# Attention and multiplicative FFN in one kernel: the fifth group turned by DMA, and every engine's order written as a list

## The chip, the cores and the metric

The kernel runs on one core of one Trainium2 chip. The metric is the time of one execution in device microseconds; a lower number is better. TensorE is called PE in the views, VectorE DVE, ScalarE ACT, GpSimd POOL and SyncE SP.

## The reference, cut to what matters

```python
q, k: 8 batches x 12 heads x 448 tokens x 64, float32; v the same
q_n = q / sqrt(mean(q*q) + 1e-6) * g_q          # k_n likewise with g_k
attn = softmax((q_n @ k_n.T) / 8)               # per head, 448 x 448
x = (attn @ v) as 3584 tokens x 768
h = ((x @ w1) * (x @ w2)) @ w3                  # 1024 wide
out = h @ w_out                                 # 3584 x 768, float32
```

## The kernel before, in words

The 96 heads go in 24 groups of four heads; three groups make a batch. A group's queries and keys are loaded (`load_qk`, L384), squared on ACT (L487), summed on DVE (L492), turned into a factor by a logarithm and an exponential on ACT (L501, L504) and scaled to bf16 on DVE (L526, two halves for queries and two for keys). They must then be turned so that the head dimension lies on partitions. That is done in one of two ways. For the first `N_PE_T = 5` groups it is done by PE: `do_turn` issues seven 128x128 transposes for the queries and seven for the keys (L1163) into a PSUM bank, and ACT or DVE copies the bank to `qkT` (L369, L373, L375), multiplying the queries by the weights `g_col` on the way. For the other 19 groups it is done by DMA: `send` (L600) issues one transposing DMA for queries and one for keys on SP's queue, and `by_g` (L534) multiplies the queries by `g_col` on DVE.

The scores of a group are seven passes (`do_score`, L716) of two PSUM banks each; ACT takes the exponential of each (L738). A pass is four concurrent matmuls over quarters of the array. When all seven are there, the value products follow, for one group or for two at once (`start_pv`, L782 and L803); ACT makes the reciprocal of the sums (L825, L826) and DVE multiplies (L845). The FFN works in pairs of PSUM banks (`Pair`, `do_pass`, L908): w pairs (w3 and w_out multiplied once into `w34s`), f pairs (x by w1, copied by ACT or DVE; x by w2, multiplied with that copy by DVE at L989 into `abT`) and o pairs (`abT` by `w34s`, copied and stored). In each pair the two row halves of the array swap banks once or more: `hand_over` (L892) puts an empty instruction on SP or POOL that waits for the last pass of the first half, and the first pass of the second half waits for it.

w3 also has to be turned by PE (`do_w3_turn`, L1185, eight transposes per block). Before there is real work PE is kept busy with warm matmuls on zeros: 512 columns (`warm`, L1360) and then 256 columns (`do_warm`, L1233).

A planner in Python runs through the whole kernel with assumed durations while the program is built and so fixes the order of instructions on every engine. On PE the rules in `pe_try` choose the next step; on ACT, DVE, SP and POOL the planner takes the job that could start first, ties by a key. The built program has no choice left: each engine executes its instructions in the written order, and semaphores hold it where data are not there.

Of the kernel before, what the change touches and what calls it, by code (L numbers as in the profile page):

```python
# [21 lines left out]
TO_ENGINE = 0.23  # L22
TO_ENGINE_WIDE = 0.45
DRAIN = 0.11
LAG = {"ACT": 0.11, "DVE": 0.09, "SP": 0.0, "POOL": 0.0}
# [3 lines left out]
BUSY = 75.0  # L29


class Job:
# [4 lines left out]
    def __init__(self, engine, took, key, emit, needs=(), done=None, moves=None):  # L37
        self.took = took if isinstance(took, dict) else {engine: took}
        self.key, self.emit, self.needs, self.done = key, emit, needs, done
        self.moves, self.any = moves, isinstance(took, dict)  # L40
# [5 lines left out]
class Planner:  # L46
# [3 lines left out]
    def __init__(self):  # L50
        self.free = {e: 0.0 for e in ("ACT", "DVE", "SP", "POOL", "PE")}
        self.jobs = []
# [5 lines left out]
    def add(self, *args, **kw):  # L58
        self.jobs.append(Job(*args, **kw))
# [37 lines left out]
    def commit(self, job, start, engine):  # L97
# [3 lines left out]
        self.jobs.remove(job)  # L101
# [28 lines left out]
    def run(self, pe_step, finished):  # L130

        stuck = 0
        while not finished() or self.jobs:
            best = None
            behind = {
                e: sum(
                    job.took[e]
                    for job in self.jobs
                    if e in job.took
                    and not job.any  # L140
                    and job.ready() <= max(self.free[e], self.now) + 0.3
                )
                for e in ("ACT", "DVE")
            }
            for e in ("ACT", "DVE", "SP", "POOL"):
                mine = []
                for job in self.jobs:
                    if e not in job.took:
                        continue
                    ready = job.ready()  # L150
                    if job.moves is not None:
                        ready = max(ready, self.lane_free(e))
                    if ready < INF:
                        at = max(ready, self.free[e], self.now)
                        if job.any and any(
                            max(ready, self.free[x], self.now) + job.took[x] + behind[x]
                            < at + job.took[e] + behind[e]
                            for x in job.took
                        ):
                            continue  # L160
                        mine.append((at, job.key, job))
                if not mine:
                    continue
                first = min(m[0] for m in mine)
                start, _, job = min(
                    (m for m in mine if m[0] <= first + 1e-9), key=lambda m: m[1]
                )
                if best is None or start < best[0]:
                    best = (start, job, e)
# [26 lines left out]
def kernel(  # L196
# [42 lines left out]
    N_PE_T = 5  # L239
# [4 lines left out]
    PAIRS = (2, 3)  # L244
    MARGINS = (0.267, 0.281)
    LOWS = (0, 2)
    VALUE_BANKS = (6, 6)
    HOLD = 0
    SOONS = (2, 4)
    STARVES = (6, 5)  # L250
    HUNGERS = (0.632, 0.85)
    ONES = (0, 0)
    FULL = (0.765, 0.208)
    PARTS = ((2, 4, 6, 8), (2, 4, 6, 8), (4, 8))
    EARLY_PAIRS = 3
    AHEAD_W3 = 3
    EARLY = 4
    STOCKS = (17, 14)
    PACES = (1.289, 1.754)
# [4 lines left out]
    SCALE_ON_ACT = ()  # L264
    LATER = 12.232
    BY_G = 0.36
    KEYS = (1.8, 1.348)
    AGAINST = (68, 115, 120, 138, 154, 245, 257, 272, 278, 299, 308, 326)
    POOL_ORDER = (
        "o0 w0 w1 w2 o1 o2 v0 u0 o3 q1 w3 w4 q2 w5 v1 u1 a0 w6 w7 v2 u2 a1 u3 v3 q3 a2 b0 b1 q4 q5 b2".split()  # L270
    )
    ON_POOL = (1, 2, 3, 4, 5)
    IN_PARTS = (6, 7, 8)
    FIRST = 3.5
    THIN_FROM = 9
    THIN = 0.627
    QUIET = 0.2

# [22 lines left out]
    used = {"a": 0, "o": 0}  # L301

    def next_of(kind):
        n = used[kind]
        used[kind] += 1
# [34 lines left out]
    qk_free = [0.0] * 3  # L340
    v_free = [0.0] * 4
# [4 lines left out]
    pv_end = [INF] * NQ  # L346
    x_at = {b: [] for b in range(B)}
# [1105 lines left out]
```

## Time and profile before

| what | value |
|---|---|
| time, median of 3 runs | 350.23 us (350.14 to 350.38) |
| span of the profiled execution | 348.0 us |
| PE busy | 342.3 us, 98% |
| ACT busy | 260.8 us, 75% |
| DVE busy | 206.7 us, 59% |
| POOL busy | 76.9 us, 22% |
| mean granted TensorE clock | 0.998 |

The span runs from the first to the last instruction; the page gives no time of its own for the profiled execution beside it. The span is 2.2 us shorter than the median time. A busy PE in this table means that a matmul was in flight, not that columns streamed without a break: ends of matmuls are modelled, and one matmul overlaps the next. Whether PE lost time is read from the starts of neighbouring passes.

### The profile page before, as it was taken

What the parts mean: (1) busy time and instruction counts of PE and PEld (TensorE: products, weight loads), DVE (VectorE), ACT (ScalarE), POOL (GpSimd) and SP (SyncE); (2) the same over time, 40 slices, a digit from 0 to 9 for tenths busy, and PEclk for the clock granted to TensorE, in tenths of its full rate; (3) what the DMA queues carried; (4) which work ended last, traced back from release to release, by engine and by line L of the source; (5) the groups of instructions that cost most, each with busy time, mean ns of one, the idle gap of its engine ahead of it and who ended that gap; (6) DMA issues with size and microseconds to landing.
All of it is one profiled execution on the core that took longest, in us unless ns stands there. A gap on an engine that the chain in (4) does not pass through costs nothing.

```text
span 348.0 us, 16174 instructions
## 1 busy us (share of the span) xinstructions
PE 342.3 (98%) x7373; PEld 219.3 (63%) x7373; DVE 206.7 (59%) x296; ACT 260.8 (75%) x371; POOL 76.9 (22%) x134
## 2 busy tenths in 40 slices
PE   8999999999999999999999999999999999999995
PEld 4767756656775756566666575566665665666674
DVE  5369289898956687486567963865894313222100
ACT  4779989999997997998799797978987882222122
POOL 8556820302222301222022022212204000000000
PEclk9999999999999999999999999999999999999999
DMA  8999999499995969948898699477898051000055
GB/s 197 206 312 204 241 299 268 89 202 199 208 187 174 92 156 188 260 107 154 148 246 161 169 165 259 116 131 186 197 185 105 7 133 53 4 2 2 4 166 155
DMA packets 68488, 55.11 MB, mean 158 GB/s; under 512 B 45060, under 2 KB 62372, under 8 KB 68420
## 3 DMA queue, kind: packets, MB, share of 16 engines
q1 hardware_dynamic: 49440, 35.33, 43.0%
q0 software_dynamic: 18048, 16.92, 29.6%
q10 hardware_dynamic: 932, 1.84, 1.4%
q8 instruction: 57, 0.93, 1.1%
q14 instruction: 11, 0.09, 0.1%
HBM read 46.66 MB, written 11.01 MB: 166 GB/s over the span
## 4 chain that ended last, share of the span: by engine, by line
PE 98%; ACT 1%; DVE 0%; issue 0%
PE ps_all L908 68%; PE ps_all L803 13%; PE ps_all L716 9%; PE ps_all L782 2%; PE ps_all L1360 2%; PE ps_all L1163 1%; PE ps_all L1185 1%; PE ps_all L1104 1%; PE ps_all L1233 1%; ACT P L738 0%; DVE abT L989 0%; ACT qk_sb L369 0%; DVE warm_t L1343 0%; PE ps_all L1373 0%
## 5 line engine op out<-in xcount | busy, mean ns | idle before, releaser
L738 ACT ACTIVATE P<-ps_all 128x896 bf16<-128x896 f32 x114 | 99.5, 916 | 11.7 <-PE ps_all L716 10.8
L424 POOL DMA_DIRECT2D v_sb<-in_v_dram x96 | 57.3, 611 | 184.1 <-PE ps_all L716 120.3
L908 PE MATMUL ps_all<-xT,w2s 64*64 64x448 bf16 x1536 | 88.5, 349 | 0.0
L908 PE MATMUL ps_all<-xT,w1s 64*64 64x448 bf16 x1536 | 86.5, 349 | 0.0
L908 PE MATMUL ps_all<-w34s,abT 64*64 64x384 bf16 x1728 | 80.2, 323 | 0.4 <-DVE abT L989 0.4
L369 ACT ACTIVATE half<-ps_all 128x896 bf16<-128x896 f32 (+1 forms) x35 | 30.6, 874 | 48.5 <-PE ps_all L908 48.3
L908 PEld LDWEIGHTS <-abT 64*64 64x64 bf16 x1728 | 51.7, 107 | 20.3 <-issue 0.7
L908 PEld LDWEIGHTS <-w2s 64*64 64x64 bf16 x1536 | 46.5, 107 | 25.6
L908 PEld LDWEIGHTS <-w1s 64*64 64x64 bf16 x1536 | 46.0, 107 | 25.7 <-issue 0.4
L716 PE MATMUL ps_all<-qkT 64*64 64x448 bf16 x672 | 60.3, 351 | 0.0
L989 DVE TENSOR_TENSOR abT<-ps_all,half 128x896 bf16<-128x896 f32 x32 | 34.8, 1089 | 41.2 <-PE ps_all L908 41.1
L492 DVE TENSOR_REDUCE ssq<-sq 128x14 f32<-128x896 f32 (+1 forms) x50 | 51.2, 1041 | 12.5 <-ACT sq L487 12.2
L526 DVE TENSOR_TENSOR qks<-qk_sb,al 128x448 bf16<-128x448 f32 x96 | 54.6, 616 | 4.8 <-ACT al L504 4.7
L487 ACT ACTIVATE sq<-qk_sb 128x896 f32<-128x896 f32 (+1 forms) x50 | 45.1, 917 | 1.6 <-DMA qk_sb<-in_q_dram 1.3
L845 DVE TENSOR_TENSOR xT<-ps_all,r 128x448 bf16<-128x448 f32 x48 | 27.5, 618 | 25.6 <-ACT r L826 22.0
L716 PEld LDWEIGHTS <-qkT 64*64 64x64 bf16 x672 | 21.7, 106 | 13.2 <-issue 4.2
L908 PE MATMUL ps_all<-w_outs,w3T 64*64 64x384 bf16 x512 | 25.1, 324 | 0.1
L803 PE MATMUL ps_all<-P,v_sb 128*32 128x448 bf16 x456 | 25.0, 352 | 0.0
L738 ACT ACTIVATE w_outs<-ps_all 128x896 bf16<-128x896 f32 x24 | 21.4, 915 | 3.2 <-PE ps_all L716 3.0
L803 PEld LDWEIGHTS <-v_sb 128*32 128x32 bf16 x592 | 15.9, 97 | 12.2 <-issue 0.2
L738 ACT ACTIVATE Pr<-ps_all 128x896 bf16<-128x896 f32 x24 | 22.1, 920 | 0.6 <-PE ps_all L716 0.5
L375 DVE COPY half<-ps_all 128x768 f32<-128x768 f32 x13 | 12.4, 955 | 12.7 <-PE ps_all L908 12.7
(63 smaller groups left out, 210.9 us busy)
## 6 DMA issues: line engine op xcount, KB each, us to landing
out_dram<-half SPq DMA_DIRECT2D x48, 192.0 KB, 3.3
qk_sb<-in_q_dram SPq DMA_DIRECT2D x15, 448.0 KB, 6.3
qk_sb<-in_k_dram SPq DMA_DIRECT2D x15, 448.0 KB, 5.4
v_sb<-in_v_dram POOLq DMA_DIRECT2D x48, 64.0 KB, 4.0
v_sb<-in_v_dram POOLq DMA_DIRECT2D x48, 48.0 KB, 4.1
qk_sb<-in_q_dram POOLq DMA_DIRECT2D x5, 448.0 KB, 8.7
qk_sb<-in_k_dram POOLq DMA_DIRECT2D x5, 448.0 KB, 9.4
w3s<-in_moe_w_dram POOLq DMA_DIRECT2D x8, 256.0 KB, 6.8
```

The lines of the kernel that those rows point to most:

```text
L369: nc.scalar.activation(out=out, in_=in_, func=AF.Copy, scale=1.0 if by is None else by)
L375: nc.vector.tensor_copy(out=out, in_=in_)
L424: nc.gpsimd.dma_start(out=v_bufs[i % 4][p0 : p0 + HP, g::2, 0 : j1 - j0].rearrange("p h j d -> p h (j d)"), in_=src[:, g::2, j0:j1].rearra ...
L487: nc.scalar.activation(out=out, in_=in_, func=AF.Square)
L492: nc.vector.tensor_reduce(out=s["ssq"][:, t, x0:x1], in_=s["sq", t][:, x0:x1], axis=AX, op=ADD)
L526: nc.vector.tensor_tensor(out=s["qks"][:, t, :, x], in0=src[:, t, x], in1=s["alpha"][:, t, x].unsqueeze(2).broadcast_to([NP, NJ, D]), op=MULT,
L716: nc.tensor.matmul(out=sc[HP * c : HP * c + HP, u, 0:S].rearrange("p (j s) -> p j s", j=NJ), lhsT=qkT[u * D : (u + 1) * D, 1, j, cols], rh ...
L738: lambda: nc.scalar.activation(out=dst, in_=sc[:, :, 0:S], func=AF.Exp),
L803: nc.tensor.matmul(out=ps_all[hd * HALF : (hd + 1) * HALF, z, 0:S], lhsT=value_weights(i, hd, j, kind), rhs=s["P"][:, hd, j, :] if j < NF ...
L845: lambda: nc.vector.tensor_tensor(out=xT[b][:, 2 * m + kind - 1, :], in0=ps, in1=s["r"], op=MULT),
L908: mm = nc.tensor.matmul(out=ps_all[64 * h : 64 * h + 64, p.bank + z, 0 : p.n], lhsT=lhsT[64 * r : 64 * r + 64, 64 * h : 64 * h + 64], rhs= ...
L989: nc.vector.tensor_tensor(out=abT[bp][:, f0 : f0 + 2, odd * S : (odd + 1) * S], in0=ps_all[:, z : z + 2, 0:S], in1=a_sb[b, f0], op=MULT,)
```

## The change

`N_PE_T` goes from 5 to 4: the group with index 4, the fifth, takes the DMA route. And the order of all five engines is written out as lists of named steps; the rules in `pe_try` are gone, the planner only follows the lists (and still picks PSUM banks, POOL or SP for a hand-over, and warm matmuls where its clock finds PE idle before 13.2 us). In `PE_ORDER` t is a turn of queries or keys, x a turn of a w3 block, s a score pass, V the start of value products, w, f and o passes of numbered pairs, L the last rows; a star gives a repeat. In the other lists s, r, a, c are square, sum, factor, scale of a group, T the copy of a turned bank, g the multiplication by `g_col`, t a transposing DMA, l a load of queries or keys, e an exponential, f and h the first copy and the multiplication of an FFN pair, O a store. The product that makes `g_col` (gp, gs) moves behind the scaling of three of the four halves of group 0, and its matmul behind the first turn.

```diff
-TO_ENGINE = 0.23
+TO_ENGINE = 0.417
+PE_ORDER = (
+    "t x0 t x1 s*2 w0*2 x2 s w0*2 w1 s w1 w0 s w0 w1*4 s w0*2 w1*2 s w1*2 w0*2 w2 w1 w2 w0*2 V1 "
+    "v*2 w2*2 w0*2 w1 w2*4 w1 w2 w1 w2 w0 w2*2 w0 w1*2 w2*4 x3 x4 t w3*4 w4 w3 w4*5 w3 w4 w3*2 w4 "
...
+    "w6*4 s w7 w6 w7*2 s w6*2 w7*2 s w7 w6*2 s w7 w6 w7 w6*3 w7*8 V2 v*8 t f0*5 f1*3 f0 f1*2 t "
+    "f0*3 f1 f0*2 s f0 f1*4 f2 f1 s f2*3 s f2*2 f1 f3*4 s f2*2 f3 f2*4 s f3 f4*2 f3*6 f5*3 s f4*4 "
...
+    "s f13*6 V2 v*8 s f14*3 s f14*3 f15*4 s f15*2 f14 s f14*4 f15 f14 s f15*5 s*4 o3*4 s o3*4 "
...
+ACT_ORDER = (
+    "s0q0 s0q1 s0k0 s0k1 a0q a0k T0q e0.0 e0.1 e0.2 e0.3 e0.4 e0.5 e0.6 n0 s1q0 s1k0 a1q w0 a1k "
...
+DVE_ORDER = (
+    "r0q0 r0q1 r0k0 r0k1 c0q0 c0q1 c0k1 gp c0k0 gs T0k x0 x1 x2 m0.1 m0.2 r1q0 r1k0 c1q0 c1q1 x3 "
...
+    "m1.1 m1.2 m2.1 m2.2 c3k0 c3k1 T3k r4q0 f0.0 r4k0 c4q1 c4q0 f0.2 c4k1 c4k0 f0.4 r5k0 r5q0 g4 "
...
+SP_ORDER = (
+    "l6k0 l6q0 l6q1 t4q t4k l7q0 l6k1 l7k0 l7k1 l7q1 t5q t5k l8q0 l8q1 l8k0 t6q l8k1 t6k l9k0 "
...
             for e in ("ACT", "DVE", "SP", "POOL"):
-                mine = []
-                for job in self.jobs:
...
+                job = self.jobs.get(ORDERS[e][self.done[e]])
+                if job is None:
+                    continue
...
-    N_PE_T = 5
+    N_PE_T = 4
...
-        p.gap_at = free[e] + 0.15
+        p.gap_at = free[e] + 0.32
...
+    def follow(t, step):
+        early, idle = idle_banks(t - WHILE), idle_banks(t)
+        idle = early + sorted((z for z in idle if z not in early), key=lambda z: bank_at[z])
+        two = adjacent(early)
+        two = adjacent(idle) if two is None else two
+        one = single(early or idle)
+        kind = step[0]
+        if kind == "s":
...
+            return do_score(t, two)
...
     def pe_step(t):
-
-        took = pe_try(t, t - MARGINS[phase()])
-        took = pe_try(t, t) if took is None else took
-        if took is None and t < WARM_TO and idle_banks(t):
+        if place[0] >= len(ORDER):
+            return None
+        took = follow(t, ORDER[place[0]])
+        if took is not None:
+            place[0] += 1
+        elif t < WARM_TO and idle_banks(t):
             return do_warm(single(idle_banks(t)))
...
-            warm(1)
+            free["PE"] = max(free["PE"], plan.now + 0.35)
...
-        warm(WARM)
+        warm(WARM + 1)
```

Three places of the built order follow; line numbers of the changed kernel differ from those of the kernel before. First SP, the queue of the loads and the transposing DMAs, behind its first loads; `qk_sb0` holds group 6 here, `qk_sb1` group 7, `qk_sb2` group 8, and `qkT_1376` of the changed kernel is group 4's. Before:

```order
L384 DMA qk_sb0_96<-in_q_dram 128x448 x2
L384 DMA qk_sb0_96<-in_k_dram 128x448 x2
L384 DMA qk_sb1_97<-in_q_dram 128x448 x2
L384 DMA qk_sb1_97<-in_k_dram 128x448 x2
L600 DMA_TRANSPOSE qkT_1637<-qks_1638 128x7x128 x2
```

Now:

```order
L473 DMA qk_sb0_96<-in_k_dram 128x448 x2
L473 DMA qk_sb0_96<-in_q_dram 128x448 x2
L693 DMA_TRANSPOSE qkT_1376<-qks_1377 128x7x128 x2
L473 DMA qk_sb1_97<-in_q_dram 128x448
L473 DMA qk_sb0_96<-in_k_dram 128x448
L473 DMA qk_sb1_97<-in_k_dram 128x448 x2
L473 DMA qk_sb1_97<-in_q_dram 128x448
L693 DMA_TRANSPOSE qkT_1619<-qks_1620 128x7x128 x2
```

In the second piece the first row also holds a load of group 0's keys. Two transposing DMAs now stand ahead of the second half of group 6's keys and of all loads of group 7.

Second DVE, at group 4 (`qks_1382` before, `qks_1377` now). Before:

```order
L526 TENSOR_TENSOR qks_1382<-qk_sb1_97,al_1351 128x7x64 x4
L375 CAST half_85<-ps_all_103 128x896
L373 TENSOR_SCALAR qkT_1381<-ps_all_103,g_col_91 128x896
L375 COPY qkT_1381<-ps_all_103 128x896
L492 TENSOR_REDUCE ssq_1502<-sq_1460 128x14
```

Now:

```order
L615 TENSOR_TENSOR qks_1377<-qk_sb1_97,al_1338 128x7x64 x2
L464 CAST half_85<-ps_all_103 128x896
L615 TENSOR_TENSOR qks_1377<-qk_sb1_97,al_1338 128x7x64 x2
L464 CAST half_85<-ps_all_103 128x896
L581 TENSOR_REDUCE ssq_1484<-sq_1435 128x14
L581 TENSOR_REDUCE ssq_1484<-sq_1455 128x14
L623 TENSOR_SCALAR qkT_1376<-qkT_1376,g_col_91 128x896
```

The two copies out of PSUM (L373, L375) are gone, one multiplication by `g_col` in SBUF has come, and an FFN copy now stands between the scaling of the queries and that of the keys.

Third DVE at the start of the kernel, where group 0 is made ready. Before:

```order
L492 TENSOR_REDUCE ssq<-sq 128x7 x2
L1366 SCALAR_TENSOR_TENSOR gp_row<-g_row 1x128
L492 TENSOR_REDUCE ssq<-sq 128x7 x2
L1381 COPY g_col<-ps_all 128x1
L526 TENSOR_TENSOR qks<-qk_sb_96,al 128x7x64 x4
```

Now:

```order
L581 TENSOR_REDUCE ssq<-sq 128x7 x4
L615 TENSOR_TENSOR qks<-qk_sb_96,al 128x7x64 x3
L1424 SCALAR_TENSOR_TENSOR gp_row<-g_row 1x128
L615 TENSOR_TENSOR qks<-qk_sb_96,al 128x7x64
L1439 COPY g_col<-ps_all 128x1
```

The product for `g_col` and the copy of its result have moved behind the scaling.

## Rows read from the trace of the kernel before

**Rows 1.** The page: busy time by engine; chain that ended last, by engine

```profile
PE 342.3 (98%) x7373; PEld 219.3 (63%) x7373; DVE 206.7 (59%) x296; ACT 260.8 (75%) x371; POOL 76.9 (22%) x134
...
PE 98%; ACT 1%; DVE 0%; issue 0%
```

**Rows 2.** Waits of PE alone: waiter <- releaser: us in total, times, longest

```profile
PE ps_all L908 <- DVE abT L989: 0.4, 1, 0.4
```

**Rows 3.** Timeline of PE, 58.0 to 60.3 us: start, busy us, instructions

```profile
57.72 1.12 PE L908 MATMUL ps_all<-xT,w1s 64*64 64x448 bf16 x20
58.77 0.95 PE L1163 MATMUL ps_all<-ident,qks 128*128 128x128 bf16 x14
59.65 0.38 PE L716 MATMUL ps_all<-qkT 64*64 64x448 bf16 x4
```

**Rows 4.** Timeline of DVE, 50 to 62 us, around group 4

```profile
57.30 1.16 DVE L526 TENSOR_TENSOR qks<-qk_sb,al 128x448 bf16<-128x448 f32 x2 [0.30 <-ACT al L504]
58.89 1.09 DVE L375 CAST half<-ps_all 128x896 bf16<-128x896 f32 x1 [0.43 <-PE ps_all L908]
```

**Rows 5.** Timeline of PE, 6.0 to 18.3 us

```profile
8.69 0.93 PE L1233 MATMUL ps_all<-warm_t 128*128 128x256 bf16 x7
9.45 0.55 PE L1163 MATMUL ps_all<-ident,qks 128*128 128x128 bf16 x7
...
11.05 0.57 PE L716 MATMUL ps_all<-qkT 64*64 64x448 bf16 x8
...
12.80 0.97 PE L908 MATMUL ps_all<-w_outs,w3T 64*64 64x384 bf16 x12
13.58 0.39 PE L716 MATMUL ps_all<-qkT 64*64 64x448 bf16 x4
13.77 0.85 PE L908 MATMUL ps_all<-w_outs,w3T 64*64 64x384 bf16 x16
14.42 0.39 PE L716 MATMUL ps_all<-qkT 64*64 64x448 bf16 x4
```

**Rows 6.** Timeline of DVE, 0 to 9.5 us, group 0 made ready

```profile
5.77 0.27 DVE L1366 SCALAR_TENSOR_TENSOR gp_row<-g_row 1x128 bf16<-1x128 f32 x1
...
7.09 2.21 DVE L526 TENSOR_TENSOR qks<-qk_sb,al 128x448 bf16<-128x448 f32 x4
```

**Rows 7.** Timeline of PE, 24 to 26 us

```profile
23.92 1.32 PE L1185 MATMUL ps_all<-ident,w3s 128*128 128x128 bf16 x16
25.08 0.55 PE L1163 MATMUL ps_all<-ident,qks 128*128 128x128 bf16 x7
```

**Rows 8.** Timelines of PE, ACT and DVE, 112.5 to 117 us

```profile
113.69 0.93 PE L908 MATMUL ps_all<-xT,w2s 64*64 64x448 bf16 x16
114.44 0.96 PE L716 MATMUL ps_all<-qkT 64*64 64x448 bf16 x12
115.81 1.33 PE L908 MATMUL ps_all<-w34s,abT 64*64 64x384 bf16 x28 [0.41 <-DVE abT L989]
...
114.02 0.95 ACT L738 ACTIVATE Pr<-ps_all 128x896 bf16<-128x896 f32 x1
...
114.67 1.09 DVE L989 TENSOR_TENSOR abT<-ps_all,half 128x896 bf16<-128x896 f32 x1 [0.23 <-PE ps_all L908]
```

**Rows 9.** Line L600, the transposing DMAs: ns min/median/max of an issue; landing

```profile
L600 SPq DMA_TRANSPOSE qkT<-qks x38: 1220/1261/2011, 68.4 to 261.8; - x38
...
DMA to landing us min/median/max: 2.6/4.0/6.1
```

**Rows 10.** Line L384 from 48 to 64 us, eight loads on SP's queue: landing

```profile
DMA to landing us min/median/max: 3.6/6.8/7.6
```

**Rows 11.** Timelines of PE, 60.5 to 66 us, and of ACT, 66 to 68 us

```profile
64.40 0.36 PE L716 MATMUL ps_all<-qkT 64*64 64x448 bf16 x4
...
66.62 0.95 ACT L487 ACTIVATE sq<-qk_sb 128x896 f32<-128x896 f32 x1
```

**Rows 12.** Line L892, the hand-overs: who waited for them: us in total, times

```profile
PEld L908: 0.2, 1
```

More of the change, by code (lines that the diff above doesn't have):

```diff
@@ L29, with unfold @@
 BUSY = 75.0
+PE_ORDER = (
[37 rows of a table added]
+)
+ACT_ORDER = (
[19 rows of a table added]
+)
+DVE_ORDER = (
[17 rows of a table added]
+)
+SP_ORDER = (
[9 rows of a table added]
+)
+POOL_ORDER = (
[8 rows of a table added]
+)
+def unfold(text):
+    return [
+        x.split("*")[0] for x in text.split() for _ in range(int((x + "*1").split("*")[1]))
+    ]
+ORDER = unfold(PE_ORDER)
+ORDERS = {
+    "ACT": ACT_ORDER.split(), "DVE": DVE_ORDER.split(),
+    "SP": SP_ORDER.split(), "POOL": POOL_ORDER.split(),
+}
 class Job:
@@ L134, in run @@
             best = None
[L135 to L144, printed above, removed]
-            for e in ("ACT", "DVE", "SP", "POOL"):
-                mine = []
-                for job in self.jobs:
[L148 to L162, printed above, removed]
-                    continue
[L164 to L169, printed above, removed]
+            for e in ("ACT", "DVE", "SP", "POOL"):
+                if self.done[e] == len(ORDERS[e]):
+                    continue
+                job = self.jobs.get(ORDERS[e][self.done[e]])
+                if job is None:
+                    continue
+                ready = job.ready()
+                if job.moves is not None:
+                    ready = max(ready, self.lane_free(e))
+                at = max(ready, self.free[e], self.now)
+                if at < INF and (best is None or at < best[0]):
+                    best = (at, job, e)
             pe_at = max(self.free["PE"], self.now)
@@ L410, in plan_load_qk @@
                     lambda which=which, x0=x0, x1=x1: load_qk(i, which, eng, x0, x1),
-                    needs=[lambda: qk_free[i % 3] + (1.0 if i > 5 else 0.0), thin],
-                    done=done, moves=(1.35 / parts, 0.086),
+                    needs=[lambda: qk_free[i] + (1.0 if i > 5 else 0.0), thin],
+                    done=done, moves=((1.1 if queue == "POOL" else 1.35) * PESS / parts, 0.086),
                 )
@@ L830, in done @@
                 s["r_at"] = e + SEM
-            add("ACT", 1.06, -1000.0, reciprocal, needs=[lambda: at], done=done)
+            add("n%d" % i, "ACT", 1.05, -1000.0, reciprocal, needs=[lambda: at, lambda: all_of(m_at[i - 2], 2) if i >= 2 else 0.0], done=done)
             return
@@ L861 @@
     running = [None]
+    made = {}
     class Pair:
@@ L1160, in do_turn @@
         )
-        took = into("t") + NJ * 0.067
+        took = into("t") + NJ * TURN
         for j in range(NJ):
@@ L1187, in do_w3_turn @@
             )
-        took += CF * 0.066
+        took += CF * TURN3
         bank_at[z] = INF
@@ L1258, in step @@
                 if z is None:
-                    z = single(idle)
+                    z = single(idle_banks(t - WHILE) or idle)
                     if z is None:
@@ L1399, with weight @@
         seq = [0]
-        def weight(emit, moves, done):
-            add("POOL", 0.6, -100.0 + seq[0], emit, done=done, moves=moves)
-        for name in POOL_ORDER:
+        def weight(name, emit, moves, done):
+            add("W" + name, "POOL", 0.6, -100.0 + seq[0], emit, done=done, moves=moves)
+        for name in LOADS.split():
             what, x = name[0], int(name[1])
```

305 lines of the change are left out of this document (131 added, 174 removed), and 81 rows, old and new, of tables (ACT_ORDER, DVE_ORDER, PE_ORDER, POOL_ORDER).

## The prediction

> **What bounds the kernel now.** I read the page first, then PE's waits, then PE's timeline. The reader should see in the page that PE has work in flight 98% of the span, and that the chain that ended last is PE for 98% too, while ACT is at 75% and DVE at 59% [rows 1]. PE's own list of waits holds 0.4 us behind the first matmul [rows 2]. That is not yet proof that no time is lost, because ends of matmuls are modelled. So I go by starts. A score pass of 448 columns takes 0.19 us (13.58 to 13.77), a product pass of 384 columns 0.16 us (four from 13.77 to 14.42) [rows 5], and nearly all starts in the timeline of PE stand at these distances. What PE has to do therefore sets the time: whatever leaves PE's list or closes a gap in it comes off the end one to one, and a step that any engine delays costs nothing until PE stands. The sum below is made on the span of 348.0 us; 2.2 us of the median, 350.23, lie around it, and I leave them as they are.
>
> **The change, part by part.**
>
> *Fourteen transposes leave PE.* They run from 58.77 to 59.65, where the next score begins: 0.88 us. Before them, five passes from 57.72 end at 58.67 (5 x 0.19), so 0.10 us more goes when PE goes over from quarter passes to full-array transposes [rows 3]. Together **-0.98 us**.
>
> *What takes their place.* Two transposing DMAs hold SP for 1.26 us each and land 2.6 to 6.1 us after their issue, 4.0 in the median [rows 9]. DVE loses two copies out of PSUM and gains one multiplication; DVE has room (59%), so I take nothing for that. The point is when PE wants the result. Before, the keys of group 4 were scaled at 57.30 + 1.16 = 58.46 [rows 4]. Now a copy of 1.09 us stands between queries and keys in DVE's order, so the keys leave SP between 58.5 and 59.6; I take 59.0, since the part of the list before it has lost nothing else. Landing is then at 61.6, 63.0 or 65.1 (shortest, median, longest). PE starts on group 4 at 64.40 now [rows 11]; all terms of this sum but the last stand ahead of it (-1.0), and the new list puts two more passes ahead (+0.38), so that moves to about 63.8. The median has 0.8 us to spare, and the longest is 1.3 us late. I take **0**, nearest to the median row, and keep 0 to +1.3 for the range. Behind the two DMAs on SP wait the second half of group 6's keys and all loads of group 7. The square of group 6's keys stood at 66.62 on ACT [rows 11]; a half load issued at about 60.5 lands 3.6 to 7.6 us later [rows 10], 64.1 to 68.1, again on either side of its use. It is the same crowd as that of the transposes, and goes into the same rival.
>
> The Trainium skill, "VectorE: DVE Perf Modes", section "The three transpose paths", gives 390 ns for a 128x128 bf16 block on TensorE and 1309 ns by DMA, and its rules take TensorE where PSUM will do. By these figures fourteen blocks cost 5.5 us on PE and 18.3 us by DMA, the keys would come some 13 us after their need, and the sum would be an estimated 362 us. The trace disagrees on both: in a stream a block holds PE for 0.06 us [rows 3], and seven blocks by DMA land in 4.0 us [rows 9].
>
> *The start.* On DVE the product for `g_col` (0.27 us at 5.77) no longer stands ahead of the sums and scales; scaling began at 7.09 with it [rows 6], and can begin about 0.2 us earlier. But the turned queries now wait for `g_col`, and between the turn of the queries and that of the keys stands a block of w3. Laid out with these durations the first score comes 0.1 us before 11.05 [rows 5]. I take **-0.1**, with -0.2 and +0.2 as bounds.
>
> *Warm matmuls.* The built order has 18 instead of 22 of 256 columns, but two of the 18 now stand singly behind the first scores. One takes 0.11 us (seven from 8.69 to 9.45) [rows 5], and two changes of array shape at 0.10 each: 0.31, twice **+0.62**. They fill time in which PE would wait. One such wait goes with them: three passes from 12.80 end at 13.29, and the next start is 13.58 [rows 5], **-0.29**.
>
> *Between 18 and 30 us.* Sixteen transposes of w3 take 1.16 us, 23.92 to 25.08, where sixteen at 0.056 take 0.90 [rows 7]: a wait of 0.25 in the middle. The list now puts three more w passes (0.49 us) between the first value products and these turns, so the wait goes: **-0.25**.
>
> *Around 114 us.* This is the largest hole. The last pass by w2 starts at 114.25, three scores follow from 114.44, and the next FFN pass needs DVE's product, which ends at 115.76; PE goes on at 115.81 instead of 115.01: 0.80 lost [rows 8]. The new list puts four scores there. The built order gives the fourth the banks of the first. A score's exponential starts 0.43 us after it (first of all: 11.05, and ACT at 11.48) and takes 0.95 [rows 8], so the fourth waits till 1.6 us after the last pass and the FFN pass till 1.8, where 0.95 would do: 0.84 lost. **+0.04**; the hole stays.
>
> *Order elsewhere.* The rest of PE's list is close to what the rules made: as many double and single value products, as many changes of array shape but for the ones counted. I take 0.
>
> The sum: -0.98 - 0.1 + 0.62 - 0.29 - 0.25 + 0.04 = -0.96, a span of 347.0 and a time of **349.3 us**.
>
> **The rivals.** About 0.2%, 0.7 us, is what a measurement of this kernel can tell from no change.
>
> *A: thin hand-overs eat the gain, no change.* Of 106 hand-overs between the row halves, the old order leaves at least 1.3 us for all but eight; the new one leaves under 0.9 us for 36, down to 0.57. For it: a hand-over stands in the queues of SP or POOL, and one behind a DMA's issue waits up to 1.26 us [rows 9]; four that hold PE for 0.25 us each, or all 36 for 0.03, give back the 0.96, and the time is 350.2. Against it: in the kernel before only one of all hand-overs was waited for by weight loads, 0.2 us [rows 12], and there 0.49 us between the last pass of one half and the first of the other sufficed. ACT's and DVE's lists, equally fixed, can do the same by small delays.
>
> *B: the turned keys come late, slower.* The eight loads on SP's queue between 50 and 60 us, with POOL's loads still running, landed after 3.6 to 7.6 us, 6.8 in the median [rows 10], where a transposing DMA in a quiet stretch needs 2.6 [rows 9]. If the fifth group's transposes are held like these loads, keys issued at 59.0 land at 65.8, 2.0 us after PE's need, and the time is 351.3; at 7.6 it is 352.1. It turns into a slowdown of over 0.7 us from a landing 6.5 us after the issue on. Against it: by 61 us the loads of the start are nearly through, and the four loads of group 7 are now behind the transposes, not beside them. The Trainium skill, "DMA: Bandwidth & Descriptors", section "Queues, rings and completion order", says that each DMA engine goes round the queues that have work, packet by packet. The trace agrees in so far as these loads took almost three times a quiet transpose's time; no row shows the same DMA with and without company.
>
> **How the numbers follow.** My forecast, 348.9 to 349.5, has 0.55: its terms are read from PE itself. A, small waits that leave between 349.5 and 350.9, has 0.28, since a fixed list on five engines has hundreds of places to lose 0.1 us and few to win. B and larger mishaps of its kind, above 350.9, have 0.17. So faster 0.55, same 0.28, slower 0.17. The range goes from 348.8 (a little more closed than counted) to 351.3, which takes in the median of B and leaves out its longest landings.
>
> **What would show it.** Right: PE has 56 transposes of queries and keys instead of 70 and none near 58 us; the first scores of group 4 follow the pass before them at 0.19 us; the hole near 114 us is still 0.8 us; no row of PE's waits is above 1 us. B: an idle of PE before a score at 64 us, put down to the qkT DMA or to the multiplication by `g_col`. A: weight loads of L908's counterpart that wait for the hand-over line for more than 0.5 us in all. The forecast is wrong altogether if new idle on PE sums to over 1 us in any other place, or if the first score comes after 11.4 us.

## The result and the profile after

The changed kernel takes **355.8 us** (353.2 to 356.8 in six runs) against 350.2 us (349.9 to 350.4): slower, ratio 1.0137 (1.0101 to 1.0173). The forecast was 349.3, with a range from 348.8 to 351.3. The profiled execution took 356.7 us with a span of 355.0, 7.0 us more than the span before. The kernels of the experiments ran later and on other chips, where the kernel before itself took 350 to 355 us, so everything there is a ratio to its runs on the same chip; where two ratios of different chips stand side by side, part of their difference can be the chips'.

The page after, the lines that answer to [rows 1]: busy time by engine, the granted clock in 40 slices, the chain that ended last.

```profile
PE 344.5 (97%) x7355; PEld 217.4 (61%) x7355; DVE 205.7 (58%) x295; ACT 260.5 (73%) x371; POOL 76.9 (22%) x134
...
PEclk9999999999998999999999999999999999999999
...
PE 93%; DMA 4%; POOL 1%; DVE 0%; issue 0%; ACT 0%; POOLq 0%
```

In the chain PE falls from 98% to 93%, and DMA and POOL stand in it for the first time. One slice, 106.5 to 115.4 us, has a granted clock below 0.9. The waits of PE, answering to [rows 2]:

```profile
PE ps_all L846 <- DMA v_sb<-in_v_dram: 2.7, 1, 2.7
PE ps_all L1418 <- DVE warm_t L1401: 1.2, 1, 1.2
PE ps_all L977 <- DVE abT L1061: 0.6, 1, 0.6
PE ps_all L797 <- ACT Pr L819: 0.6, 1, 0.6
PE ps_all L977 <- issue: 0.3, 1, 0.3
```

The first row is new: a value product waits 2.7 us for a load (2.86 us by starts). (The third, 0.6 us at 269.7, is an FFN product whose operand DVE delivers late: its scaling by `g_col` ahead of it waited 0.8 us for a transposing DMA.) The timeline of PE there, and the stretches around it (columns after the times: busy time of each engine, granted clock, DMA share, GB/s):

```profile
104.57 0.38 PE L846 MATMUL ps_all<-Pr,ones 64*32 64x448 bf16 x8
104.77 0.35 PE L846 MATMUL ps_all<-Pr,v_sb 64*32 64x448 bf16 x2
107.84 0.57 PE L846 MATMUL ps_all<-Pr,v_sb 64*32 64x448 bf16 x14 [2.72 <-DMA v_sb<-in_v_dram]
108.34 1.66 PE L867 MATMUL ps_all<-P,ones 128*32 128x448 bf16 x24
109.77 3.47 PE L867 MATMUL ps_all<-P,v_sb 128*32 128x448 bf16 x40
```

```profile
105.00:108.00 3.00, 0.28 (x10) 0.14 (x14) 1.81 (x3) 0.00 (x0) 0.00 (x0) 1.00 1.25 151
108.00:112.70 4.70, 4.70 (x74) 2.10 (x64) 0.98 (x2) 2.97 (x5) 0.00 (x0) 0.64 0.39 145
112.70:116.00 3.30, 3.30 (x72) 1.85 (x68) 2.42 (x4) 1.73 (x2) 0.09 (x1) 1.00 0.00 0
```

PE stood from 105.0 to 107.8. From 109.4 to 112.4 eight passes start 0.37 us apart, where such passes take 0.19 elsewhere: the granted clock of that stretch is 0.64, so part of it ran at 1.2 instead of 2.4 GHz, after PE had done almost nothing for 2.8 us. By 112.7 it is back at 1.00.

Where the 7.0 us went, by starts of neighbouring passes as in the prediction:

| piece | us |
|---|---|
| what PE has to do: -0.98 transposes, +0.62 warm matmuls | -0.36 |
| waits at 13.3 and 24.5 us, gone as forecast | -0.54 |
| value load late at 105 to 108 us | +2.86 |
| passes at the low clock behind it | +1.6 |
| FFN product held on DVE at 269.7 us | +0.77 |
| gap at 43.15 us with no semaphore (below: code) | +0.45 |
| rest, by difference: small gaps, the hole at 120 us -0.03 | +0.9 |
| first score, 11.05 to 11.17 | +0.12 |
| last pass to the end, 4.16 to 5.33 | +1.17 |

Why the load is late is seen on POOL. First the kernel before, then the changed one: issues of value pieces, with their number and what the queue had waited for.

```profile
78.83 1.79 POOL L424 DMA_DIRECT2D v_sb<-in_v_dram  x3 [11.38 <-PE ps_all L908]
87.93 2.38 POOL L424 DMA_DIRECT2D v_sb<-in_v_dram  x4 [7.31 <-PE ps_all L716]
97.13 2.38 POOL L424 DMA_DIRECT2D v_sb<-in_v_dram  x4 [6.81 <-PE ps_all L716]
```

```profile
79.30 4.15 POOL L513 DMA_DIRECT2D v_sb<-in_v_dram  x7 [7.65 <-PE ps_all L797]
97.55 2.98 POOL L513 DMA_DIRECT2D v_sb<-in_v_dram  x5 [14.10 <-PE ps_all L797]
```

The view of the line L513 from 97 to 101 us, then that of the hand-overs, L961, from 83 to 98 us:

```profile
L513 POOL DMA_DIRECT2D v_sb<-in_v_dram x5: 597/622/642, 97.5 to 99.9; - x5
...
DMA to landing us min/median/max: 4.9/6.0/7.9
```

```profile
L961 POOLq EVENT_SEMAPHORE  x4: 17/17/17, 90.5 to 96.9; - x4
```

Before, the last pieces of groups 6 and 7 went out at 88 to 90 us. Now they are the fourth and fifth of the piece list `v8.1 v8.2 v8.0 v7.3 v6.2`, issued at 99.3 and 99.9 us, and the last lands at 107.8. Their own buffers were free long before; they stand behind group 8's pieces, and these behind four hand-overs in POOL's queue, which wait for PE's passes at 90.5 to 96.9 us. (The rows above put the queue's idle time down to a score pass, but each of these batches starts 0.5 to 0.6 us behind the last hand-over ahead of it: 78.69 and 79.30, 96.94 and 97.55 in the changed kernel, 87.33 and 87.93 in the one before.) These loads went out no earlier than the last empty instruction in front of them.

### The profile page after: what moved, and what is told of

It reads as the page before. It is cut to its first block, busy times and chain, and to the rows that moved or that the text cites. A ratio compares the mean times of both kernels' runs of the same rounds, so it can differ in the third digit from the quotient of the medians.

```text
span 355.0 us, 16117 instructions
## 1 busy us (share of the span) xinstructions
PE 344.5 (97%) x7355; PEld 217.4 (61%) x7355; DVE 205.7 (58%) x295; ACT 260.5 (73%) x371; POOL 76.9 (22%) x134
## 4 chain that ended last, share of the span: by engine, by line
PE 93%; DMA 4%; POOL 1%; DVE 0%; issue 0%; ACT 0%; POOLq 0%
PE ps_all L977 64%; PE ps_all L867 13%; PE ps_all L797 9%; DMA v_sb<-in_v_dram 2%; PE ps_all L846 2%; PE ps_all L1418 2%; DMA qkT<-qks 1%; PE ps_all L1257 1%; PE ps_all L1235 1%; PE ps_all L1176 1%; POOL v_sb L513 1%; PE ps_all L1344 1%; DVE abT L1061 0%; ACT Pr L819 0%; DVE qk_sb L464 0%
## 5 line engine op out<-in xcount | busy, mean ns | idle before, releaser
L819 ACT ACTIVATE P<-ps_all 128x896 bf16<-128x896 f32 x114 | 99.2, 919 | 11.2 <-PE ps_all L797 10.1
L513 POOL DMA_DIRECT2D v_sb<-in_v_dram x96 | 57.3, 621 | 188.5 <-PE ps_all L977 103.6
L977 PE MATMUL ps_all<-xT,w2s 64*64 64x448 bf16 x1536 | 97.4, 349 | 0.6 <-DVE abT L1061 0.6
L977 PE MATMUL ps_all<-xT,w1s 64*64 64x448 bf16 x1536 | 97.0, 349 | 0.0
L977 PE MATMUL ps_all<-w34s,abT 64*64 64x384 bf16 x1728 | 82.7, 322 | 0.0
L977 PEld LDWEIGHTS <-w1s 64*64 64x64 bf16 x1536 | 45.0, 107 | 26.1 <-issue 0.4
L867 PE MATMUL ps_all<-P,v_sb 128*32 128x448 bf16 x456 | 26.8, 368 | 0.0
```

The source lines that it names most:

```text
L513: nc.gpsimd.dma_start(out=v_bufs[i % 4][p0 : p0 + HP, g::2, 0 : j1 - j0].rearrange("p h j d -> p h (j d)"), in_=src[:, g::2, j0:j1].rearra ...
L819: lambda: nc.scalar.activation(out=dst, in_=sc[:, :, 0:S], func=AF.Exp),
L867: nc.tensor.matmul(out=ps_all[hd * HALF : (hd + 1) * HALF, z, 0:S], lhsT=value_weights(i, hd, j, kind), rhs=s["P"][:, hd, j, :] if j < NF ...
L977: mm = nc.tensor.matmul(out=ps_all[64 * h : 64 * h + 64, p.bank + z, 0 : p.n], lhsT=lhsT[64 * r : 64 * r + 64, 64 * h : 64 * h + 64], rhs= ...
```

## The experiments

**Late value pieces.** First the two pieces moved to the front:

```diff
-    "v8.1 v8.2 v8.0 v7.3 v6.2 v9.0 v8.3 v9.2 v11.0
+    "v7.3 v6.2 v8.1 v8.2 v8.0 v9.0 v8.3 v9.2 v11.0
```

> Theory L (late values): the changed kernel's loss is one value load. In POOL's list the last pieces of groups 6 and 7 stand behind three pieces of group 8, whose buffer is free only when the products of groups 3 and 4 are through at 97.5 us; the last piece lands at 107.8 us and PE, which wants it at 105.0, stands for 2.86 us and then makes nine passes at 0.37 instead of 0.19 us (1.65 us). With the two pieces ahead of group 8's, both go: 355.8 - 4.5 = 351.3 us, and the profile has no gap above 0.8 us on PE. Rival P (slow passes of their own): the passes at 0.37 us come from something else, crowded transfers or the products' own load, and stay at 108 to 112 us: 355.8 - 2.9 = 352.9. Rival D (crowded transfers): the pieces that come out of the queue 98 to 104 us take 5 to 8 us to land whoever is first, so another piece or group 8's keys are late instead: 354.5 to 355.8.

Measured: ratio 1.0032 (1.0006 to 1.0058), profiled span 350.7. Nine pieces go out together, and PE runs through its products at 0.19 us:

```profile
80.10 5.33 POOL L513 DMA_DIRECT2D v_sb<-in_v_dram  x9 [7.65 <-PE ps_all L797]
98.54 1.79 POOL L513 DMA_DIRECT2D v_sb<-in_v_dram  x3 [13.11 <-PE ps_all L797]
```

```profile
105.77 0.56 PE L846 MATMUL ps_all<-Pr,v_sb 64*32 64x448 bf16 x16
106.26 1.32 PE L867 MATMUL ps_all<-P,ones 128*32 128x448 bf16 x24
107.40 1.88 PE L867 MATMUL ps_all<-P,v_sb 128*32 128x448 bf16 x36
```

The two pieces landed at 87.9 and 90.0 us, some 16 us before their use. The wait and the low clock went together, so P and D fall for this place, and the ratio is the one that L gives (351.3 to 350.2). Two things in the expectation were wrong. A gap above 0.8 us was left, 0.92 us by starts at 49.4 us (below: code). And group 8's buffer was not what the queue waited for (the products that held it were through by 77 us); it waited for the hand-overs, as above. Two runs go with it:

```diff
-    "v8.1 v8.2 v8.0 v7.3 v6.2
+    "v8.1 v7.3 v6.2 v8.2 v8.0
```

> The two pieces stay behind the wait for the buffer, but only one piece of group 8 stands ahead of them: they are issued at about 98.2 and 98.8 us instead of 99.3 and 99.9 and land, by the five rows of the changed kernel (5.1, 4.9, 6.2, 6.0, 7.9 us after issue, in this order), at 103.0 to 104.9 us, where PE wants them at 105.0. Theory L: no wait or one below 0.4 us, and no pass at 0.37 us behind it: the profile is 4.0 to 4.5 us shorter than the changed kernel's 356.7, at 352.2 to 352.7. Rival P: no wait, but the slow passes stay: 353.8. If the clock falls after any wait, however short, some nine passes at 0.37 us remain as well.

Measured: one execution, 353.1 us, no wait at 106 us (the later of the two pieces landed at 105.5, for a use at 106.6) and no slow pass. That is as L has it, but the next run, with the list unchanged, has no wait of this kind either; so this execution does not show what two places in the queue are worth. The changed kernel once more:

> The changed kernel, unchanged, for its time and a second look at the gap. Theory L, put right by the last trace: the two value pieces wait behind four hand-overs in POOL's queue, the last of which PE releases at 97 us. Then the gap of 2 to 3 us at 105 to 108 us and the passes at 0.37 us behind it are here again, and the time is 3.5 to 4.5 us above that of the run with the pieces ahead (ratio to the kernel before 1.012 to 1.016). If the gap was an accident of one execution, it is not here and the ratio is 1.003 to 1.005.

Measured: ratio 1.0071 (1.0030 to 1.0112), and in the profiled execution (353.3 us) no gap at 105: the five pieces went out at 98.6 to 100.9 us and the last landed at 105.75, after 4.8 instead of 7.9 us, just in time for a use at 105.8 to 106.0:

```profile
98.60 2.98 POOL L513 DMA_DIRECT2D v_sb<-in_v_dram  x5 [14.40 <-PE ps_all L797]
...
DMA to landing us min/median/max: 4.8/5.1/5.3
```

The ratio lies between the two that were expected. **The 4.5 us are not in every execution**; the list left no reserve, and the landing decides from run to run. The third of group 5's pieces stood as close. On top of e1's edit, with one store moved as in e5 below:

```diff
-    v4.1 v4.3 v4.2 v5.1 v5.3 v6.1 v5.2 v6.0
+    v4.1 v4.3 v4.2 v5.1 v5.2 v5.3 v6.1 v6.0
-    O3.1.0 O3.2.0 O3.4.0 O3.3.0 O3.5.0
+    O3.1.0 O3.2.0 O3.3.0 O3.4.0 O3.5.0
```

> The value pieces of groups 6 and 7 ahead of group 8's, the store of the fourth tile ahead of the fifth's, and one more value piece moved: the third of group 5 stands two places further ahead in POOL's list (it went out at 80 us, landed at 84.0 to 87.0 in five runs, and PE wanted it at 84.6 to 86.1). Theory L, several late values: the gap of 0.27 to 1.00 us inside group 5's products at 85 us is gone, the other gaps stay, ratio 1.0015 to 1.0030. Rival E (elastic): the time gained is lost behind it, ratio 1.003 to 1.004.

Measured: ratio 1.0010 (0.9982 to 1.0038); the gap at 85 us is gone from the trace. The ratio is a little below L's range, but it is from another chip than e1's 1.0032 and the intervals overlap, so it doesn't tell L from E. A gap of 0.5 us opened at 55 us.

**Small gaps one by one.** Both runs are on top of e1's edit.

```diff
-    c23k0 f5.4 g22 h5.4 g23 h5.6
+    c23k0 f5.4 h5.4 g22 h5.6 g23
-    w7 w6*2 s w7 w6 w7 w6*3 w7*8 V2
+    w7 w6*2 s w7 w6*4 w7*9 V2
```

> The values as in the run before it, and two lists altered: on DVE the multiplication by g_col of group 22 no longer stands ahead of an FFN product (PE stood 0.77 us at 269.7 us), and on PE three more passes stand between the row halves of the last w3 pair (0.45 us at 43.15). Theory L with these gaps counted one to one: 1.2 us below the run with the value pieces ahead, 350.1. Rival E (elastic): ACT or the transfers set the pace behind these places, and half of it or more comes back as waits further on: 350.5 to 351.3.

Measured: ratio 1.0046 (1.0023 to 1.0070), not below e1's on the same chip. The two gaps are gone, but they were hardly there in e1 either (0.2 us and none); others stood there, 0.7 us at 50 us (0.9 in e1), 1.0 at 87 (0.3 in e1) and 0.7 at 154 (none in e1; below: code). A gap read from one execution of these lists need not be in the next.

```diff
-    e2.6 s3k0 a3q w7 n1 n2 a3k
+    e2.6 s3k0 w7 a3q n1 n2 a3k
```

> The value pieces ahead, and two lists altered: on SP the store of the fourth tile of the last batch no longer stands behind that of the fifth (it was issued 2.3 us after its partner on ACT, 3 us before the end, so nine stores instead of eight were on their way at the end), and on ACT the copy of the folded weights stands ahead of the scale of group 3's queries, which waits for a load (PE stood 0.65 to 1.12 us at 49 to 50 us in four runs). Theory S: the end comes 4.2 us behind the last pass instead of 5.0, and the gap at 49 us is below 0.3: together 1.2 to 1.6 us below the run with the value pieces ahead, ratio 0.999 to 1.000. Rival E (elastic): one gap closes and the next one opens, the ratio stays at 1.002 to 1.004.

Measured: ratio 1.0035 (1.0009 to 1.0062), as rival E has it. In the trace half of theory S came true. The stores: the last lands 3.44 us behind the last pass, where it was 4.03 in the changed kernel, 3.75 in e1 and 3.16 in the kernel before. The rows of the last stores, changed kernel, then this one, then the kernel before:

```profile
DMA to landing us min/median/max: 3.1/3.5/3.9
```

```profile
DMA to landing us min/median/max: 2.6/2.8/3.1
```

```profile
DMA to landing us min/median/max: 2.3/2.4/2.5
```

From the last landing to the end it is 1.3 us in these two runs of the new lists and 1.0 in the kernel before. That 0.3 does not belong to the lists: it is 1.34 us in e3 and e6, which have none of them, and 0.92 in e4, which has them; what it is stays open. The gap at 49 us was still there, 1.11 us, with ACT's reciprocals done in time: ACT was not its cause.

**The DMA turn by itself.** The fifth group back on PE in the repaired lists:

```diff
-    N_PE_T = 4
+    N_PE_T = 5
-    f3 f4*2 f3*6 f5*3 s f4*4
+    f3 f4*2 f3*6 f5*2 t t f5 s f4*4
-    f0.4 r5k0 r5q0 g4
+    f0.4 r5k0 T4q T4k r5q0
-    l6q1 t4q t4k l7q0
+    l6q1 l7q0
```

> The values ahead, and the fifth group's queries and keys turned on PE again, fourteen transposes at about 60.5 us, with their two copies on DVE and without the two transposing DMAs on SP. Theory of the prediction: fourteen transposes and one change of shape cost PE 0.98 us one to one and the DMAs cost nothing: 351.3 + 1.0 = 352.3. Rival F: without the two DMAs SP's loads behind them come 2.5 us earlier and a wait elsewhere shortens, or the transposes fall into a wait: 351.3 to 351.8. Rival G: the scores of group 4 wait for the copies on DVE, which stand among its sums: 352.8 or more.

Measured: ratio 1.0059 (1.0031 to 1.0087) against e1's 1.0032 on the same chip: 0.27%, 0.95 us more, the size forecast, with intervals as wide as the difference. (By the medians it is 1.6 us, and in the profiled executions 0.7 us of the difference lies ahead of the first score.) Then one number in the kernel before:

```diff
-    N_PE_T = 5
+    N_PE_T = 4
```

> The kernel before with its rules, and one number changed: groups 0 to 3 are turned on PE instead of 0 to 4. The fifth group's fourteen transposes are gone from PE and no list is fixed; the rules then build another order behind that place. What PE has to do falls by 0.98 us. Theory of the prediction (the turn by DMA is free): 0.9 to 1.0 us faster, ratio 0.997 to 0.998. Rival B (the turned keys come late): PE stands at 60 to 66 us for 1 us or more and the ratio is 1.000 or above. Rival C (chance of the order): the order that the rules make behind that place has gaps of its own anywhere, and the ratio is anything from 0.997 to 1.005 with the gaps elsewhere than at 60 to 66 us.

Measured: ratio 1.0246 (1.0210 to 1.0282). The rules built another order behind 58 us, with fourteen scores at 80 to 91 us, waits for their exponentials there and again a run of passes at the low clock behind a wait of 2.2 us. That is rival C in kind, though far dearer than its 1.005, and so no test of the turn. That needs the old order kept:

```diff
+            if i == 4:
+                nc.sync.dma_start_transpose(out=s["qkT"][:, t], in_=...)
...
-        for j in range(NJ):
+        for j in range(NJ if i < 4 else 0):
```

> The kernel before with its order kept to the letter on every engine, its rules still reckoning with the fifth group's turn on PE, but the fourteen transposes not issued: two transposing DMAs go out on SP as soon as the queries and keys are scaled (ahead of group 6's keys), the two copies leave DVE and the multiplication by g_col stands behind the next sum. So the DMA turn alone, without a new order. Theory of the prediction: the turn costs nothing and 0.98 us of PE's list goes: ratio 0.9970 to 0.9980 (350.2 to 349.2). Rival B: the keys leave SP at about 60 us and PE wants them at 63.4; a landing after 4.0 us, the median, is 0.6 us late: ratio 0.9985 to 0.9995; after 6.8 us it is 1.002 or above. If the order that the rules made was the cause of the 8.6 us in the run with one number changed, nothing of that shows here.

Measured: ratio 1.0023 (0.9994 to 1.0051), no gain; the forecast, 0.9970 to 0.9980, lies outside. The keys were not late: they landed at 63.2 us, and the first score of group 4 at 65.05 waited for nothing. But of the 0.98 us, 1.05 are given back before it: 0.29 at 59.5, where a score waits for ACT's exponential, 0.27 at 62.8, where one waits for ACT's FFN copy, and 0.49 at 64.3, where passes wait for a hand-over that stands on SP behind the transposing DMAs and the loads and runs at 64.2 (in this kernel's own numbering the passes are L924 and the hand-overs L908):

```profile
PE ps_all L924 <- SPq L908: 0.3, 1, 0.3
```

> The kernel before, unchanged, for its profile on the chip of these runs. If the late first score (11.5 to 12.2 us in the four runs behind us, 11.05 before) and the end 5.0 us behind the last pass (4.16 before) belong to the chip, they show here too; if they belong to the new lists, the first score is at 11.0 to 11.1 and the end 4.2 us behind the last pass.

Measured: first score 11.22 us, end 4.34 us behind the last pass, time 350.0. So this execution has neither the late first score nor the long end. But e3 and e6, without the new lists, have the first score at 11.55 and 11.77 us and the end 4.4 and 4.6 us behind the last pass, where runs of the new lists have 11.2 to 12.2 and 4.65 to 5.3. The late first score does not belong to the lists; of the end, the part that the order of the stores makes does, as e5 showed.

**A gap without a semaphore.** Eight profiled executions with the new lists and their old number of warm matmuls (e1, e1b, e2, e4, e5, e7, e9 and after_again) show 0.65 to 1.12 us at 49 us, in the middle of a product; the first profile of the changed kernel has 0.45 at 43 us instead. Here that of e1:

```profile
47.71 0.74 PE L867 MATMUL ps_all<-half,v_sb 128*32 128x448 bf16 x12
48.28 0.36 PE L867 MATMUL ps_all<-P,v_sb 128*32 128x448 bf16 x4
49.39 0.56 PE L867 MATMUL ps_all<-P,v_sb 128*32 128x448 bf16 x8 [0.74 <-issue]
```

This pass waits for no semaphore. Counted in the trace, matrix multiplies and weight loads together, it is always PE's 1,730th instruction; the gap at 43 us, in the changed kernel, is at the 1,474th. In e3, where the work at these places is another, there are gaps at both, 1.3 us at the 1,474th and 0.6 at the 1,730th. 256 instructions lie between them, and the gaps of 0.7 us at 154 us in e2 and 0.5 us at 151.6 us in e5 are at the 6,082nd, 17 times 256 further on. The page's row for code says why that is a distance to notice:

```profile
q8 instruction: 57, 0.93, 1.1%
```

57 pieces in 0.93 MB are 16 KB each, and for the 14,733 instructions of PE in the trace that makes 258 per piece. The DMA view by stretch shows when one comes: in the kernel before (before_again) between 44 and 46.5 us, in the changed one (after_again) between 46.5 and 48, with the engines full of POOL's loads.

```profile
q8 instruction: 1, 0.02, 2.4%
```

```profile
q0 software_dynamic: 113, 0.41, 102.1%
q8 instruction: 1, 0.02, 5.0%
```

The Trainium skill, "Runtime: NRT & Kernel Launch", section "Instruction fetch mechanics", says that an engine's program streams in blocks of 256 instructions over a DMA queue of its own, and that the crossing of a block is mostly hidden. The trace agrees on the blocks; hidden the crossing is in the kernel before, and not in most runs of the new lists. The traces also hold the packet of each piece, and with it the time when the piece had landed (us):

| run | piece landed | 1,730th instruction starts | between | lost before it |
|---|---|---|---|---|
| kernel before | 45.89 | 47.58 | 1.69 | none |
| e6 | 46.45 | 48.16 | 1.71 | none |
| e8 (below) | 45.31 | 47.44 | 2.13 | none |
| e1 | 48.09 | 49.39 | 1.29 | 0.9 |
| e3 | 48.97 | 50.34 | 1.37 | 0.6 |
| after_again | 47.79 | 49.28 | 1.50 | 1.0 |
| e12 (below) | 47.23 | 48.66 | 1.43 | 0.9 |

In all eleven executions with a gap at this instruction it starts 1.29 to 1.51 us after the piece landed, wherever in time that is; the kernel before has 0.2 to 0.4 us to spare. The test adds 32 instructions ahead of everything and no work (on e7's lists, as is e9 below):

```diff
-            for _ in range(n):
-                    out=ps_all[:, 7, :], ..., rhs=warm_t,
+            for _ in range(2 * n):
+                    out=ps_all[:, 7, 0:256], ..., rhs=warm_t[:, 0:256],
```

> The same lists, but each of the sixteen warm matmuls of 512 columns at the start is two of 256, so all later instructions of PE stand 32 places further on in its program and nothing else changes. Theory C (code): the gap of 0.65 to 1.12 us at 49 us, with no wait on a semaphore, behind the first pass of the seventh product of groups 1 and 2, is PE out of instructions: they come in pieces of 16 KB over a queue of their own and the piece lands when PE is nearly through the one before. Then the gap comes 32 instructions, four passes, earlier: behind the first pass of the sixth product, or behind the last of the fifth. Rival W (a wait of data or of a bank that the trace does not name): the gap stays at the same pass, behind the first of the seventh product.

Measured: one execution, 350.54 us, and no gap at all near 49 us: neither answer. (The piece had landed 2.1 us ahead of its use.) Less traffic was tried beside it:

```diff
-    l3q0 v3.3 v3.0 v3.2 v2.3 Wa2
+    l3q0 v2.3 Wa2
-    Wb2 v5.0 v3.1
+    Wb2 v3.3 v3.0 v3.2 v5.0 v3.1
```

> The lists of the run with group 5's value piece moved, and three value loads of group 3 (wanted at 72 us) put behind the last weights: 0.16 MB less on their way at 35 to 42 us, when the pieces of code for 43 and 49 us are fetched. Theory C with the crowd as its cause: the piece that landed at 47.1 to 48.5 us lands by 46.5, the gap at 49 us is below 0.3 us, ratio 0.6 to 1.0 us below the run without this edit. Rival: the transfers are at their limit from 30 to 58 us in any case and the piece lands no earlier; the gap stays, or the value loads of group 3 are themselves late at 72 us.

Measured: ratio 1.0010 (0.9982 to 1.0038), the gap 0.80 us at the same instruction; the piece landed at 47.3, 1.5 us before the instruction starts. The rival holds in this execution: that much less traffic did not close the gap. Then both together, timed, and the shift on the changed kernel alone:

> The lists of the run with the later values, and the code shifted by 32 places, now timed. Theory C (code pieces): the gap of 0.8 us at 49 us is gone as in the one look; ratio 1.000 (0.998 to 1.001), against 1.001 for the run with the later values. Rival (that look was a lucky execution): the gap at 49 us is back, four passes earlier or where it was, and the ratio is 1.001 to 1.003.

> The changed kernel with its lists as they were, and only the code shifted by 32 places. If code pieces carry most of its loss: ratio 1.003 or below and no gap at 43 to 50 us. If late value pieces carry it (theory L): the gaps at 85 us and 105 to 108 us stay, the ratio is 1.005 to 1.012, at most 0.003 below the 1.0071 and 1.0137 measured for the changed kernel.

Measured: e11 **0.9992** (0.9965 to 1.0019), no gap at 49 us; e12 **1.0070** (1.0037 to 1.0104). The trace of e12 gives the answer that e8 did not:

```profile
47.16 0.74 PE L867 MATMUL ps_all<-P,v_sb 128*32 128x448 bf16 x12
48.66 0.75 PE L867 MATMUL ps_all<-half,v_sb 128*32 128x448 bf16 x12 [0.76 <-issue]
49.23 0.76 PE L867 MATMUL ps_all<-P,v_sb 128*32 128x448 bf16 x12
```

The gap now stands behind the last pass of the fifth product instead of the first of the seventh: four passes, 32 instructions earlier, as Theory C had it. It stays with the instruction's number, not with the work. With the landing times in the table that shows it: PE waits for its code there. Whether a piece comes in time changes from one execution to the next: e11 and e8 have no gap, e12 and e10 have one with the same shift. What makes it late is not shown.

e12 against e11, on one chip, is what the late value pieces (groups 5, 6 and 7), group 3's moved pieces and the store cost together: 0.78%, 2.7 us by the timed runs, against 2.5 to 4.8 us that the changed kernel lost in its own (1.0071 and 1.0137). The runs do not split it among the four; e12's runs spread from 352.0 to 357.6, and its profiled one, 352.7, is among the shortest, with 0.17 us twice of waits for values. The shift alone bought nothing that can be measured (1.0070 against 1.0071).

**The hole at 115 to 120 us.** On e11's lists:

```diff
-    s f15*5 s*4 o3*4 s o3*4 o4*5 s
+    s f15*5 s*2 o3*6 s*2 o3*2 s o4*5 s
...
+            if t == NT // 2 and bp == 0:
+                part = ab_at[1][: pos // 2 + 1]
+                return max(all_of(w34_at, CF), all_of(part, pos // 2 + 1)) + SEM
```

> All that closed a gap so far (value pieces of groups 5, 6 and 7 earlier, those of group 3 later, the store of the fourth tile in its turn, code shifted by 32 places), and the hole at 115 to 120 us attacked: the fourth tile's pair of the FFN's second half reads the last product of DVE only in its last two positions, but the rule let it start when the whole tile was there. Now six of its passes (0.98 us) stand where the third and fourth score stood, and these scores behind them. Theory H (the hole is only a rule): the gap of 0.77 us there goes to below 0.2; 0.6 to 0.8 us below the run with the code shifted, ratio 0.998 to 0.999, faster than both kernels. Rival E (elastic): the two scores that come 1 us later leave ACT without work there and their exponentials are waited for behind it; ratio as in the run with the code shifted.

Measured: ratio 1.0011 (0.9982 to 1.0040), no better than e11. The 0.77 us are gone at their place, and 0.70 and 0.62 come 2 us later, where PE waits for exponentials; 1.02 us opened ahead of it, at 111.75, where ACT's square waited 2.0 us for a key load with the exponentials behind it (in e11 it did not wait; the edit lies behind this place):

```profile
PE ps_all L797 <- ACT P L819: 0.5, 1, 0.5
...
PE ps_all L977 <- ACT P L819: 0.4, 1, 0.4
```

Part of this is rival E: ACT stood 0.53 us at 116.4 for the score that comes later now, and PE then waited for the exponentials. But the late key load had put ACT 1.1 us behind e11's before the edit could act, so this trace does not say what the hole would be without it, and that the hole is ACT's pace is not shown; by the times the edit brings no gain. No version beat both kernels: e11 beats the changed one by 0.8% and equals the one before.

## Why the prediction was wrong

**The step that failed** is the last of the sum: "*Order elsewhere.* ... I take 0." It compared PE's list with itself, products against products, and left out POOL's. There the pieces of groups 6 and 7 had been put behind group 8's and behind hand-overs; that cost 2.86 us and some 1.6 of low clock in the profiled execution, nothing in that of after_again and 0.2 us in that of e12. With this alone moved out of the way the ratio was 1.0032 (e1), against 1.0137 and 1.0071 of the changed kernel on other chips; with the smaller edits between e12 and e11 it was worth 2.7 us. The order of all five lists was open before the run, and so was the place of the pieces in POOL's list. With the issues at 99.3 and 99.9 us that the trace then showed, the longest landing of a load in [rows 10], 7.6 us, ends at 107.5, 2.5 us behind the use; of such a sum the prediction has nothing.

*Fourteen transposes, -0.98.* PE's list is shorter by that. That a shorter list "comes off the end one to one" was the general premise, and it doesn't hold by itself: with the old order kept (e6) 1.05 us come back as waits for ACT (0.56) and for a hand-over (0.49). In the new lists (e4) the 0.95 us agree with it, within wide intervals.

*What takes their place, 0.* Right in the profiled execution, and partly by luck. The keys left SP at 59.85 us (59.0 forecast) and landed at 62.5; the first score of group 4 followed its pass at 0.19 us, at 64.59:

```profile
DMA to landing us min/median/max: 2.7/3.2/3.8
```

```profile
63.08 1.68 PE L977 MATMUL ps_all<-xT,w2s 64*64 64x448 bf16 x32
64.59 0.36 PE L797 MATMUL ps_all<-qkT 64*64 64x448 bf16 x4
```

So rival B is false here. But 2.7 us is the shortest of the keys' landings: in the eleven other executions of lists with this turn it is 4.1 to 5.4 us, which leaves from 0.9 us down to nothing before the score, and in e2 the score came 0.4 us late:

```profile
PE ps_all L797 <- DMA qkT<-qks: 0.2, 1, 0.2
```

And e6's hand-over, late on SP behind the two DMAs, is a price that this term left out. *The start, -0.1.* Measured +0.12; from the first square to the first score it is 0.15 shorter, but the queries landed 0.27 later. *Warm matmuls, +0.62 and -0.29*, and *the wait at 24.5 us, -0.25*: right, the two single fillers stand at 11.68 and 13.54 and both waits are gone. *The hole, 0.84*: measured 0.77.

```profile
119.05 0.80 PE L797 MATMUL ps_all<-qkT 64*64 64x448 bf16 x12
120.43 0.38 PE L797 MATMUL ps_all<-qkT 64*64 64x448 bf16 x4 [0.58 <-ACT Pr L819]
```

*The end* has no term in the sum; it was 4.16 us behind the last pass and grew by 1.17, of which 0.87 lie ahead of the last store's landing.

*Rival A, thin hand-overs.* Small in the first profile, not always: the weight loads' waits for SP's hand-overs there, and in the changed kernel's second profile.

```profile
PEld L977 <- SPq L961: 0.3, 1, 0.3
```

```profile
PEld L977 <- SPq L961: 1.4, 2, 1.2
```

Its mechanism, a fixed list that leaves little room, is close to what happened; its price was too low because it was put on hand-overs that PE waits for, and not on what stands behind them in the same queue. What the forecast would have been wrong by, it named ("new idle on PE sums to over 1 us in any other place"); it gave that case too small a chance.

## What to carry to other kernels

When a change writes out the order of every engine, check each queue of loads against the stage that uses it: issue time, plus the longest landing of its kind, against the use, with what stands in front of it in that queue, empty instructions too. Work taken off the busiest engine counts only as far as the other engines and queues follow; with the old order ACT and one hand-over took a whole microsecond back. And judge small gaps from several executions: one trace shows where a list is thin, not what it costs. A gap with no semaphore is worth counting in instructions.

## What the runs showed of the hardware

- PE waits for its own code: gaps of 0.35 to 1.3 us at fixed places of its program, multiples of 256 instructions apart, that move by 32 instructions when 32 are put in front. At the 1,730th each of eleven gaps ends 1.29 to 1.51 us after the piece of code landed; without a gap that time is up to 2.1 us. Moving 0.16 MB of loads out of the way did not close the gap in the one run that tried it.
- A wait of 2.86 us on PE was followed by eight passes at half speed, 0.37 instead of 0.19 us, at a granted clock of 0.64 over 4.7 us; one of 2.2 us in e3 likewise (0.62 over 4.5 us), while waits of 1.1 us (e4, e5) were followed by passes at 0.19.
- The same value piece from the same place in the queue landed after 7.9 and after 4.8 us in two executions of one program.
- A transposing DMA of the same keys from the same place in SP's list landed after 2.7 us in one execution of the changed kernel and after 4.3 us in the next.
